# A list scheduler's table of durations and hops, replaced in a fused attention, expert and feed-forward kernel

## The chip, the cores and the metric

One core of one Trainium2 chip runs the whole kernel. The metric is the device time in microseconds (us). The time before is 1770.32 us, the median of three runs (1769.96 to 1772.51). The profile comes from one execution, with five engines: TensorE (PE) multiplies matrices, VectorE (DVE) and ScalarE (ACT) do element work, GpSimd (POOL) helps them, SyncE (SP) starts the transfers.

## The reference

Three stages follow each other, in float32, for 4 batches of 576 rows, 8 heads of 64:

```python
# attention without a seq x seq matrix; each half has its own softmax
q_s = exp(q - max(q, -1));  q_s /= sum(q_s, -1) + 1e-9        # over a row's 64 values
k_s = exp(k - max(k, seq)); k_s /= sum(k_s, seq) + 1e-9       # over the 576 rows
x   = einsum('bhsd,bhde->bhse', q_s, einsum('bhsd,bhse->bhde', k_s, v))   # -> 2304 x 512
# 8 experts, all of them for all rows; the gate is balanced 8 times
P = exp(x @ w_gate - max)
for _ in range(8):
    P /= P.sum(1, keepdims=True) + 1e-9;  P /= P.sum(0, keepdims=True) + 1e-9;  P *= 2304 / 8
y = sum(P[:, e:e+1] * (relu(x @ w1[e]) @ w2[e]) for e in range(8))        # 512 -> 1024 -> 512
# feed-forward with a hard swish
h = y @ w_in;  out = (h * clip(h + 3, 0, 6) / 6) @ w_out                  # 512 -> 2048 -> 512
```

## The kernel before, in words

The arithmetic is float32 made of float16 pieces: an operand is scaled by a power of two and split into a high and a low float16 part, and a product is three float16 products. The large products are done by blocks with seven block products in place of eight, so there are many sums and differences of blocks to form ahead of PE and behind it. Weights come to `raw`, are split by ACT (the high part) and DVE (the low part, a `scalar_tensor_tensor`, STT below) into `w1buf_79`/`w1buf_80` and `w2buf_81`/`w2buf_82`, and are ready one slice ahead of their use. Tokens come in strips of 384: a product `b<-xbuf,w1buf` is six matmuls of 128x384 into one of eight PSUM banks (`b_61` to `b_68`); ACT and DVE gather the banks into `ring_r`, split `ring_r` into `ring_h`, and the second products read `ring_h` and go to `acc`. Attention is done in two pairs of batches. The second pair's preparation lies beside the first expert work: the maximum of k over the sequence is a chain of four `tensor_max` on DVE (2048, 1024, 512 and 512 wide, out in `scr`; marked `1kmax`), four PE transposes of `scr` (`1ktr`), a reduction to `ring_c_109`, eight PE products with `units` that spread the result over the rows (`1kback`), two wide subtractions on DVE (`xbuf<-xbuf,b`, 2304 wide; `1ksub`), exponentials on ACT (`1kexp`) and a burst of 64x64 products on PE. The scale of a weight slice needs a sum of squares (ACT), a product with `identb` on PE that brings the partitions' values together (`b<-identb,ring_c`), and small DVE operations into `ring_ws`.

No engine reorders at run time: each executes its instructions in the order of the program. That order is worked out by the class `Planner`, in which every operation is first recorded, with what it reads and writes. `cost` (L177) gives an operation a duration from its shape; `hop` (L286) the time between the end of one operation and the start of a dependent one on another engine; `order` (L295) walks backwards to a due time for each operation, shifted for some by the tables EARLIER and LATER, and calls `lay` (L317) twice. `lay` is a list scheduler: it keeps the time at which each engine is free, takes the engine whose best ready operation can start first, and of operations that can start within 30 ns of each other the one due first. Its first pass lays what is not marked as fill; the second lays everything, and a fill operation (weight preparation, conversion of w_in and w_out) goes in where `following` finds that it delays nothing due. DVE and POOL operations that share a port carry a lock, and in the plan they exclude each other. `issue` (L444) then emits all in the planned order, and, in the plan's first 130 us, puts small filler matmuls (`b<-units,plus`, L2385) where the plan sees PE pause for over 400 ns, called warm in the code; they have no result. So the planned times decide nothing but the order and the fillers' number. What waits for what on the chip is set by semaphores.

Of the kernel before, what the change touches and what calls it, by code (L numbers as in the profile page):

```python
# [73 lines left out]
class Planner:  # L74
# [7 lines left out]
    HOP = 120.0  # L82
    MARGIN = 300.0
    NEAR = 4000.0
# [92 lines left out]
    def cost(self, eng, name, out, ins):  # L177
# [4 lines left out]
        if eng == "tensor":  # L182
            passes = 1.0
            if out.dtype == F32 and ins[0].dtype == F32:
                passes = 2.0 if name == "transpose" else 4.0 if ins[0].shape[0] > 64 else 1.5
            return 2.0 + n * 0.4167 * passes
        if eng == "scalar":
            return 170 + 0.8 * n if psum else (720 if n == 512 else 180 + 0.9 * n)
# [7 lines left out]
        if eng == "gpsimd":  # L196
            if big == 512 and len(out.shape) > 2:
                return 1610
            return 70 + (2.25 if len(ins) > 1 else 1.2) * big
# [86 lines left out]
    def hop(self, a, b):  # L286
        if a["eng"] == b["eng"] and a["eng"] != "sync":
            return 0.0
        if a["eng"] == "tensor":
            return 170.0 + self.HOP  # L290
        if a["eng"] == "sync":
            return a.get("land", 2500.0 + a["dma"] / 150.0)
        return self.HOP + (self.MARGIN if b["eng"] == "tensor" else 0.0)

# [22 lines left out]
    def lay(self, ops, first):  # L317
# [8 lines left out]
        lag = shift = pipe = 0.0  # L326
        gone = set()
# [14 lines left out]
        def following(q, t, d):  # L342
# [5 lines left out]
            for o in reversed(q[-24:]):  # L348
# [10 lines left out]
                u += o["dur"]  # L359
                v += o["dur"]  # L360
# [5 lines left out]
        def pick(e):  # L366
            f = free[e]
            c = []
            for o in waits[e]:
# [3 lines left out]
                if first and o["fill"] and e != "sync" and o["late"] + lag > s + self.NEAR:  # L373
                    room, fits = following(e, s, o["dur"])
                    if not fits:
                        s = max(s + 50.0, room + 1.0)
                    elif o["lock"]:
                        room, fits = following(other[e] + " lock", s, o["dur"])
                        if not fits:
                            s = max(s + 50.0, room + 1.0)  # L380
# [5 lines left out]
            if e not in ("tensor", "sync"):  # L386
                end = s + o["dur"]
# [5 lines left out]
        while len(result) < len(ops):  # L393
# [19 lines left out]
            end = s + o["dur"] * (1.0 if e == "tensor" else 1.05)  # L413
            if e == "sync":
                free[e] = s + 500.0
                pipe = max(pipe, s + 2000.0) + o["dma"] / 370.0
                o["land"] = pipe + 1500.0 - s
                end = s
            else:
                free[e] = end  # L420
            if o["lock"]:
                lock[e] = end
# [1996 lines left out]
```

## Time and profile before

| | |
|---|---|
| Runs (median, lowest, highest) | 1770.32, 1769.96, 1772.51 us |
| Span of the profiled execution, first to last instruction | 1768.3 us |
| PE busy | 1750.0 us (99%) |
| DVE busy | 1411.4 us (80%) |
| ACT busy | 1251.0 us (71%) |
| POOL busy | 588.0 us (33%) |
| Mean granted PE clock | 0.999 |

The page gives the profiled execution by its span; the median of the runs is 2.0 us above that, which is the start and the end around the instructions. A row of a timeline gives the start, the length and the number of instructions of a group; the length reaches to the modelled end of the last one. Since matmuls are pipelined, the start of the next row is often a better mark than the end of the last: six matmuls of 128x384 have a length of 1.14 us, and six more start 0.98 us behind them. An idle time stands in brackets behind a row, with what ended it. Filler matmuls count as busy in all views, so a stretch in which PE waits can read as 100% busy; they are told apart by their line, L2385.

### The profile page before, as it was taken

Reading aid. Unit: us, or ns where it says so; the run is one execution under the profiler, and the core shown is the slowest. Engines: PE = TensorE matmul, PEld = TensorE weight load, DVE = VectorE, ACT = ScalarE, POOL = GpSimd, SP = SyncE. Lnnn points to the kernel's source line nnn. Section 1 sums busy time; section 2 is a strip of 40 time slices with the busy share of each in tenths; the row PEclk is TensorE's granted clock in tenths of the full one; section 3 lists DMA queues with packets and bytes.
Section 4 is the critical chain, followed back from the end, with each engine's and each line's share of the span. In section 5 each row is a group of like instructions: output and inputs, shape, how many; then the busy total and the mean of one; then the engine's idle time right before and its main releaser. Section 6 shows DMA issues by size and latency. Waiting matters only on the chain.

```text
span 1768.3 us, 33908 instructions
## 1 busy us (share of the span) xinstructions
PE 1750.0 (99%) x13199; PEld 1218.1 (69%) x13199; DVE 1411.4 (80%) x2629; ACT 1251.0 (71%) x2807; POOL 588.0 (33%) x651
## 2 busy tenths in 40 slices
PE   7999999999999999999999999999999999999999
PEld 5555556777777777777777777777777555777776
DVE  7874877787888888888888888888888788777884
ACT  5856575667667686777778687768777677767673
POOL 3423343434444423232333322333323223223311
PEclk9999999999999999999999999999999999999999
DMA  9410322324242313020303122130312454402022
GB/s 293 121 69 1 117 84 74 99 98 154 98 161 96 111 37 105 25 87 25 119 21 119 37 93 63 49 105 25 105 49 93 87 100 136 150 25 87 1 87 84
DMA packets 103330, 154.25 MB, mean 87 GB/s; under 512 B 47744, under 2 KB 51840, under 8 KB 102912
## 3 DMA queue, kind: packets, MB, share of 16 engines
q1 hardware_dynamic: 103168, 152.08, 27.8%
q8 instruction: 103, 1.69, 0.4%
q14 instruction: 59, 0.48, 0.1%
HBM read 119.69 MB, written 24.12 MB: 81 GB/s over the span
## 4 chain that ended last, share of the span: by engine, by line
PE 96%; DVE 2%; issue 1%; DMA 1%; ACT 0%; POOL 0%; SPq 0%; DVEq 0%; POOLq 0%; ACTq 0%
PE b L472 95%; PE b L2385 1%; DMA xbuf<-in_k_dram 0%; DVE prob L472 0%; DVE acc L472 0%; DVE ring_r L472 0%; DVE xbuf L472 0%; DMA acc<-in_q_dram 0%; DVE ring_rs L472 0%; SPq L472 0%; ACT w2buf L472 0%; DVE scr L472 0%; DVE ring_cs L472 0%; POOL wtmp L472 0%; DVE ring_c L472 0%
## 5 line engine op out<-in xcount | busy, mean ns | idle before, releaser
L472 PE MATMUL b<-xbuf,w1buf 128*128 128x384 f16 x5040 | 910.6, 326 | 0.4 <-DVE ring_r L472 0.2
L472 PEld LDWEIGHTS <-w1buf 128*128 128x128 f16 x5040 | 491.5, 98 | 278.2 <-issue 1.8
L472 PE MATMUL b<-w2buf,ring_h 128*128 128x256 f16 (+2 forms) x3048 | 523.5, 308 | 0.0
L472 POOL TENSOR_TENSOR ring_h<-ring_r,ring_h 128x384 f16<-128x384 f32 x262 | 259.8, 993 | 693.4 <-ACT ring_h L472 632.7
L472 PEld LDWEIGHTS <-ring_h 128*128 128x128 f16 x3810 | 371.4, 98 | 155.9 <-issue 1.8
L472 ACT COPY b<-b 128x256 f32<-128x256 f32 (+1 forms) x686 | 253.8, 376 | 191.5 <-PE b L472 114.6
L472 DVE SCALAR_TENSOR_TENSOR acc<-b,ring_cf,acc 128x512 f32<-128x512 f32 x372 | 270.9, 746 | 120.7 <-PE b L472 94.3
L472 PEld LDWEIGHTS <-xbuf 128*128 128x128 f16 x3228 | 303.2, 98 | 75.5 <-DVE xbuf L472 1.1
L472 ACT ACTIVATE ring_r<-b 128x384 f32<-128x384 f32 x319 | 155.2, 488 | 94.9 <-PE b L472 87.7
L472 DVE SCALAR_TENSOR_TENSOR ring_r<-b,ring_r 128x384 f32<-128x384 f32 x215 | 118.7, 553 | 65.3 <-PE b L472 37.6
L472 PE MATMUL b<-xbuf 128*128 128x256 f16 (+1 forms) x1338 | 118.8, 251 | 2.2 <-issue 1.6
L472 POOL TENSOR_TENSOR raw<-raw 128x256 f32<-128x256 f32 (+1 forms) x119 | 102.0, 874 | 52.7 <-DVE w2buf L472 18.9
L472 POOL TENSOR_TENSOR ring_h<-scr,ring_h 128x384 f16<-128x384 f32 x40 | 38.8, 970 | 225.2 <-ACT ring_h L472 216.6
L472 ACT ACTIVATE ring_h<-ring_r 128x384 f16<-128x384 f32 x210 | 108.2, 521 | 7.7 <-DVE ring_r L472 5.4
L472 PE MATMUL b<-scr,xbuf 128*128 128x256 f16 x762 | 107.2, 273 | 0.1
L472 PE MATMUL b<-w2buf,xbuf 128*128 128x256 f16 x762 | 107.2, 273 | 0.0
L472 PE MATMUL b<-kvs,xbuf 128*128 128x256 f16 x762 | 107.2, 273 | 0.0
L472 PE MATMUL b<-xbuf,ring_h 128*128 128x256 f16 x468 | 91.2, 273 | 0.0
L472 DVE SCALAR_TENSOR_TENSOR acc<-b,ring_co,acc 128x512 f32<-128x512 f32 (+1 forms) x82 | 60.3, 741 | 27.5 <-PE b L472 25.7
L472 DVE TENSOR_TENSOR xbuf<-scr,xbuf 128x384 f16<-128x384 f32 x126 | 76.9, 635 | 6.5 <-ACT xbuf L472 6.3
L472 DVE SCALAR_TENSOR_TENSOR w1buf<-raw,ring_ws,w1buf 128x512 f16<-128x512 f32 x100 | 79.2, 825 | 3.1 <-ACT w1buf L472 2.7
L472 ACT ACTIVATE scr<-b 128x384 f32<-128x384 f32 x113 | 54.8, 488 | 37.2 <-PE b L472 36.6
(197 smaller groups left out, 2128.2 us busy)
## 6 DMA issues: line engine op xcount, KB each, us to landing
xbuf<-xkeep SPq DMA_DIRECT2D x119, 384.0 KB, 3.5
raw<-in_moe_w_dram SPq DMA_DIRECT2D x31, 1024.0 KB, 5.5
scr<-in_moe_w_in_dram SPq DMA_DIRECT2D x13, 512.0 KB, 3.7
scr<-in_moe_w_out_dram SPq DMA_DIRECT2D x12, 512.0 KB, 3.4
xkeep<-xbuf SPq DMA_DIRECT2D x2, 2688.0 KB, 9.0
xkeep<-xbuf SPq DMA_DIRECT2D x14, 384.0 KB, 8.4
out_dram<-acc SPq DMA_DIRECT2D x18, 256.0 KB, 2.0
raw<-win SPq DMA_DIRECT2D x4, 1024.0 KB, 5.4
```

The costliest lines, as they stand in the source:

```text
L472: f(*a, **k)
L2385: real.tensor.matmul(banks[t][:, : 2 * P], plus, some, start=True, stop=True, skip_group_check=True)
```

## The change

The table of durations and hops gets other numbers, and the scheduler tells two times apart. (1) The hop from DVE or ACT to another engine goes from 120 to 45 ns, from POOL to 95; a result for PE still adds MARGIN, 300 ns. From PE to another engine it is 165 ns and the hop of the receiver (45, or 95 for POOL), in place of 290. (2) `held`, which is new, is the time for which an operation keeps its engine (and the lock): its duration less 80 ns on DVE and ACT or 40 ns on POOL, times 1.01. Its result is there after the whole duration. Before, both were the duration times 1.05. (3) Durations: ACT's formula loses its special case at 512 and adds 90 ns for each further input; POOL's is 320+1.6n with two inputs and 220+0.88n with one, where it was 70+2.25n and 70+1.2n; PE's products on 64 rows get shorter. DVE's formula stays. (4) Transfers: at most eight are under way in the plan, with another rate and another latency. The operations are the same, 9017 in both; EARLIER and LATER stay, and the fillers go from 131 to 132.

```diff
@@ -79,8 +79,11 @@
...
     SLACK = 60000.0
-    HOP = 120.0
+    HOP = {"vector": 45.0, "scalar": 45.0, "gpsimd": 95.0, "tensor": 65.0, "sync": 120.0}
+    OVERLAP = {"vector": 80.0, "scalar": 80.0, "gpsimd": 40.0}
+    IN_FLIGHT = 8
     MARGIN = 300.0
+    SLOW = 1.01
@@ -182,10 +185,12 @@
...
             if out.dtype == F32 and ins[0].dtype == F32:
-                passes = 2.0 if name == "transpose" else 4.0 if ins[0].shape[0] > 64 else 1.5
+                passes = 2.0 if name == "transpose" else 4.0 if ins[0].shape[0] > 64 else 0.78
+            elif ins[0].shape[0] <= 64:
+                passes = 0.3
...
         if eng == "scalar":
-            return 170 + 0.8 * n if psum else (720 if n == 512 else 180 + 0.9 * n)
+            return (170 + 0.8 * n if psum else 180 + 0.88 * n) + 90 * (len(ins) - 1)
@@ -194,9 +199,7 @@
...
         if eng == "gpsimd":
-            if big == 512 and len(out.shape) > 2:
-                return 1610
-            return 70 + (2.25 if len(ins) > 1 else 1.2) * big
+            return 320 + 1.6 * big if len(ins) > 1 else 220 + 0.88 * big
@@ -287,10 +290,13 @@
...
         if a["eng"] == "tensor":
-            return 170.0 + self.HOP
+            return 165.0 + self.HOP[b["eng"]]
...
             return a.get("land", 2500.0 + a["dma"] / 150.0)
-        return self.HOP + (self.MARGIN if b["eng"] == "tensor" else 0.0)
+        return self.HOP[b["eng"]] + (self.MARGIN if b["eng"] == "tensor" else 0.0)
+
+    def held(self, o):
+        return max(o["dur"] - self.OVERLAP.get(o["eng"], 0.0), 40.0) * (1.0 if o["eng"] == "tensor" else self.SLOW)
@@ -324,6 +330,7 @@
...
         lag = shift = pipe = 0.0
+        landed = []
@@ -356,8 +363,8 @@
...
                     break
-                u += o["dur"]
-                v += o["dur"]
+                u += self.held(o)
+                v += self.held(o)
@@ -371,11 +378,11 @@
...
                 if first and o["fill"] and e != "sync" and o["late"] + lag > s + self.NEAR:
-                    room, fits = following(e, s, o["dur"])
+                    room, fits = following(e, s, self.held(o))
...
                     elif o["lock"]:
-                        room, fits = following(other[e] + " lock", s, o["dur"])
+                        room, fits = following(other[e] + " lock", s, self.held(o))
@@ -384,7 +391,7 @@
...
             if e not in ("tensor", "sync"):
-                end = s + o["dur"]
+                end = s + self.held(o)
@@ -410,16 +417,19 @@
...
             o["start"] = s
-            end = s + o["dur"] * (1.0 if e == "tensor" else 1.05)
+            end = s + o["dur"]
             if e == "sync":
+                if len(landed) >= self.IN_FLIGHT:
+                    s = max(s, landed[-self.IN_FLIGHT])
                 free[e] = s + 500.0
-                pipe = max(pipe, s + 2000.0) + o["dma"] / 370.0
-                o["land"] = pipe + 1500.0 - s
+                pipe = max(pipe, s + 1900.0) + o["dma"] / (310.0 if s < 4500.0 else 385.0)
+                landed.append(pipe + 200.0)
+                o["land"] = landed[-1] - s
...
             else:
-                free[e] = end
+                free[e] = s + self.held(o)
             if o["lock"]:
-                lock[e] = end
+                lock[e] = free[e]
...
             if e == "tensor":
```

Since the plan's numbers changed, most rows of the program change places: 1278 of PE's 2776 operations, 2378 of DVE's 2629, 2239 of ACT's 2628, 483 of POOL's 645 and 170 of SP's 339. Three places follow. In these rows a name such as `b_62<-xbuf,w1buf_79` is the tile written and the tiles read, and a count at the end means equal rows in succession.

PE, four transposes of the second pair's k maximum (`b_67<-units,scr`). Before, they stand late in the first expert work, between products with `w1buf_80`:

```order
L472 LDWEIGHTS w1buf_80
L472 MATMUL b_61<-xbuf,w1buf_80 128x384
L472 MATMUL b_67<-units,scr 128x128 x4
L472 LDWEIGHTS w1buf_80
L472 MATMUL b_62<-xbuf,w1buf_80 128x384
```

Now they stand behind a product with `w1buf_79` and two fillers:

```order
L482 LDWEIGHTS w1buf_79
L482 MATMUL b_62<-xbuf,w1buf_79 128x384
L2395 LDWEIGHTS plus
L2395 MATMUL b_68<-units,plus 128x256
L2395 LDWEIGHTS plus
L2395 MATMUL b_68<-units,plus 128x256
L482 MATMUL b_67<-units,scr 128x128 x4
L482 LDWEIGHTS w1buf_79
L482 MATMUL b_62<-xbuf,w1buf_79 128x384
```

The four transposes moved ahead of some twenty product groups; they keep their place in front of the eight products that spread the maximum.

DVE, the maximum's last two steps and the splits of `w1buf_80`. Before:

```order
L472 TENSOR_TENSOR scr<-scr 128x8x64
L472 SCALAR_TENSOR_TENSOR w1buf_80<-wtmp,ring_ws,w1buf_80 128x512
L472 SCALAR_TENSOR_TENSOR w1buf_80<-raw,ring_ws,w1buf_80 128x512
L472 SCALAR_TENSOR_TENSOR w1buf_80<-wtmp,ring_ws,w1buf_80 128x512
L472 SCALAR_TENSOR_TENSOR ring_r<-b_62,ring_r 128x384
L472 TENSOR_SCALAR ring_ws<-ring_c1i 128x1
L472 SCALAR_TENSOR_TENSOR w2buf_81<-acc,ring_ws,w2buf_81 128x512 x2
L472 SCALAR_TENSOR_TENSOR ring_r<-b_63,ring_r 128x384
L472 SCALAR_TENSOR_TENSOR ring_r<-b_62,ring_r 128x384
L472 SCALAR_TENSOR_TENSOR w2buf_81<-acc,ring_ws,w2buf_81 128x512 x2
L472 SCALAR_TENSOR_TENSOR w1buf_80<-raw,ring_ws,w1buf_80 128x512 x2
L472 TENSOR_TENSOR scr<-scr,xbuf 128x512
```

Now the maximum's last three steps (`scr<-scr 128x8x128`, `scr<-scr 128x8x64`, `scr<-scr,xbuf 128x512`) stand here, ahead of the splits:

```order
L482 TENSOR_REDUCE ring_c_108<-b_67 128x1
L482 TENSOR_TENSOR scr<-scr 128x8x128
L482 SCALAR_TENSOR_TENSOR ring_r<-b_62,ring_r 128x384
L482 TENSOR_SCALAR ring_c_108<-ring_c_108 128x1
L482 TENSOR_TENSOR scr<-scr 128x8x64
L482 SCALAR_TENSOR_TENSOR ring_h<-ring_r,ring_h 128x384
L482 TENSOR_SCALAR ring_c1i<-ring_c_108 128x1
L482 TENSOR_TENSOR scr<-scr,xbuf 128x512
L482 TENSOR_SCALAR ring_ws<-ring_c1i 128x1 x2
L482 SCALAR_TENSOR_TENSOR ring_r<-b_62,ring_r 128x384
```

and the splits stand around the two wide subtractions (`xbuf<-xbuf,b_68 128x2304`):

```order
L482 SCALAR_TENSOR_TENSOR w1buf_80<-raw,ring_ws,w1buf_80 128x512
L482 SCALAR_TENSOR_TENSOR w2buf_81<-acc,ring_ws,w2buf_81 128x512
L482 SCALAR_TENSOR_TENSOR w1buf_80<-wtmp,ring_ws,w1buf_80 128x512
L482 SCALAR_TENSOR_TENSOR w1buf_80<-raw,ring_ws,w1buf_80 128x512
L482 SCALAR_TENSOR_TENSOR ring_r<-b_62,ring_r 128x384
L482 TENSOR_TENSOR xbuf<-xbuf,b_68 128x2304
L482 SCALAR_TENSOR_TENSOR ring_r<-b_62,ring_r 128x384
L482 SCALAR_TENSOR_TENSOR ring_r<-b_63,ring_r 128x384
L482 TENSOR_TENSOR xbuf<-xbuf,b_68 128x2304
L482 SCALAR_TENSOR_TENSOR w1buf_80<-wtmp,ring_ws,w1buf_80 128x512
```

The two subtractions stood behind the splits and now stand ahead of the fourth `w1buf_80` split of this slice.

DVE in the middle of the expert stage, from the splits of the next slice's weights (`w1buf_79<-raw`) to the gather of `b_62` into `scr`, which frees a bank for PE. Before:

```order
L472 SCALAR_TENSOR_TENSOR ring_r<-ring_r 128x384
L472 SCALAR_TENSOR_TENSOR w1buf_79<-raw,ring_ws,w1buf_79 128x512
L472 SCALAR_TENSOR_TENSOR ring_r<-ring_r 128x384
L472 TENSOR_SCALAR ring_ws<-ring_c1i 128x1
L472 SCALAR_TENSOR_TENSOR w1buf_79<-raw,ring_ws,w1buf_79 128x512 x2
L472 SCALAR_TENSOR_TENSOR acc<-b_67,ring_cf,acc 128x512
L472 SCALAR_TENSOR_TENSOR acc<-b_66,ring_cf,acc 128x512
L472 SCALAR_TENSOR_TENSOR scr<-b_62,scr 128x384
L472 SCALAR_TENSOR_TENSOR w1buf_79<-raw,ring_ws,w1buf_79 128x512 x2
L472 TENSOR_TENSOR ring_r<-scr,ring_r 128x384
```

and now:

```order
L482 TENSOR_TENSOR xbuf<-ring_r,xbuf 128x384
L482 TENSOR_SCALAR ring_c1i<-ring_c_108 128x1
L482 TENSOR_TENSOR xbuf<-ring_r,xbuf 128x384
L482 TENSOR_SCALAR ring_ws<-ring_c1i 128x1
L482 TENSOR_TENSOR xbuf<-ring_r,xbuf 128x384
L482 TENSOR_TENSOR ring_r<-ring_r 128x384
L482 TENSOR_SCALAR ring_ws<-ring_c1i 128x1
L482 SCALAR_TENSOR_TENSOR w1buf_79<-raw,ring_ws,w1buf_79 128x512
L482 SCALAR_TENSOR_TENSOR acc<-b_67,ring_cf,acc 128x512
L482 SCALAR_TENSOR_TENSOR acc<-b_66,ring_cf,acc 128x512
L482 SCALAR_TENSOR_TENSOR w1buf_79<-raw,ring_ws,w1buf_79 128x512 x4
L482 SCALAR_TENSOR_TENSOR scr<-b_62,scr 128x384
```

The gather stood behind three of these splits and two `acc` additions, and now stands behind five of them, three `xbuf` subtractions and a sum as well.

## Rows read from the trace of the kernel before

**Rows 1.** The page: PE's busy time, and the chain that ended last.

```profile
PE 1750.0 (99%) x13199; PEld 1218.1 (69%) x13199; DVE 1411.4 (80%) x2629; ACT 1251.0 (71%) x2807; POOL 588.0 (33%) x651
...
PE 96%; DVE 2%; issue 1%; DMA 1%; ACT 0%; POOL 0%; SPq 0%; DVEq 0%; POOLq 0%; ACTq 0%
```

**Rows 2.** By stretch: start:end, length, each engine's busy us (instructions), clock, DMA.

```profile
0.00:20.00 20.00, 9.21 (x57) 6.15 (x58) 12.54 (x24) 5.77 (x12) 4.27 (x9) 0.96 0.93 331
...
20.00:40.00 20.00, 19.57 (x425) 15.26 (x422) 14.79 (x36) 15.98 (x25) 12.96 (x11) 0.95 0.92 240
...
40.00:60.00 20.00, 20.00 (x141) 12.83 (x140) 18.82 (x40) 17.97 (x44) 6.01 (x7) 1.00 0.82 231
...
800.00:1000.00 200.00, 199.99 (x1536) 149.82 (x1535) 168.23 (x305) 150.74 (x357) 62.96 (x70) 1.00 0.20 61
```

**Rows 3.** Timeline of PE, 49-72 us: start, length, line, operation, count.

```profile
51.91 0.60 PE L2385 MATMUL b<-units,plus 128*128 128x256 f16 x4
...
56.30 0.38 PE L2385 MATMUL b<-units,plus 128*128 128x256 f16 x2
...
58.52 0.71 PE L2385 MATMUL b<-units,plus 128*128 128x256 f16 x5
...
61.02 0.60 PE L2385 MATMUL b<-units,plus 128*128 128x256 f16 x4
...
67.31 4.05 PE L472 MATMUL b<-w2buf,ring_h 128*128 128x512 f16 x18
```

**Rows 4.** Timeline of DVE, 52 to 88 us.

```profile
52.42 1.37 DVE L472 TENSOR_TENSOR scr<-scr 128x1024 f32<-128x1024 f32 x1
...
58.67 0.75 DVE L472 SCALAR_TENSOR_TENSOR w1buf<-raw,ring_ws,w1buf 128x512 f16<-128x512 f32 x1
...
59.34 0.68 DVE L472 TENSOR_TENSOR scr<-scr 128x512 f32<-128x512 f32 x1
...
69.24 1.21 DVE L472 TENSOR_TENSOR scr<-scr,xbuf 128x512 f32<-128x512 f32 x1
...
82.67 5.02 DVE L472 TENSOR_TENSOR xbuf<-xbuf,b 128x2304 f32<-128x2304 f32 x2
```

**Rows 5.** Timeline of ACT, 52 to 57 us.

```profile
54.75 0.63 ACT L472 ACTIVATE w1buf<-raw 128x512 f16<-128x512 f32 x1
...
56.28 0.52 ACT L472 ACTIVATE ring_h<-ring_r 128x384 f16<-128x384 f32 x1
```

**Rows 6.** Timeline of POOL, 68 to 70 us.

```profile
68.73 1.17 POOL L472 TENSOR_TENSOR raw<-raw,wtmp 128x256 f32<-128x256 f32 x1
```

**Rows 7.** Timeline of PE, 78 to 95 us.

```profile
78.98 0.60 PE L472 MATMUL b<-units,scr 128*128 128x128 f32 x4
...
81.46 1.09 PE L472 MATMUL b<-units,ring_c 128*64 128x128 f32 x16
...
93.77 1.45 PE L472 MATMUL b<-xbuf 64*64 64x65 f32 x83 [1.55 <-issue]
```

**Rows 8.** Timeline of PE at the balancing of the gate.

```profile
205.99 0.39 PE L472 MATMUL b<-ring_cs,units 128*128 128x8 f32 x2 [0.28 <-DVE ring_cs L472]
...
210.15 0.39 PE L472 MATMUL b<-ring_cs,units 128*128 128x8 f32 x2 [0.51 <-DVE ring_cs L472]
```

**Rows 9.** Timeline of PE in the expert stage.

```profile
867.61 0.27 PE L472 MATMUL b<-lg,ring_h 128*128 128x256 f16 x1
...
879.74 1.14 PE L472 MATMUL b<-xbuf,w1buf 128*128 128x384 f16 x6
```

**Rows 10.** Timeline of DVE in the expert stage.

```profile
868.53 1.41 DVE L472 SCALAR_TENSOR_TENSOR acc<-b,ring_cf,acc 128x512 f32<-128x512 f32 x2 [1.14 <-ACT b L472]
...
877.00 1.41 DVE L472 SCALAR_TENSOR_TENSOR acc<-b,ring_cf,acc 128x512 f32<-128x512 f32 x2 [0.23 <-PE b L472]
...
878.33 0.55 DVE L472 SCALAR_TENSOR_TENSOR scr<-b,scr 128x384 f32<-128x384 f32 x1
```

**Rows 11.** The page's costliest groups: DVE's sums of 384.

```profile
L472 DVE SCALAR_TENSOR_TENSOR ring_r<-b,ring_r 128x384 f32<-128x384 f32 x215 | 118.7, 553 | 65.3 <-PE b L472 37.6
```

## The prediction, made before the changed kernel ran

> **What bounds the kernel now.** I read the page's busy times and chain first, then the busy time by stretch, then the timelines of PE, DVE and ACT in the stretches where PE does not run through. PE is busy for 1750.0 of 1768.3 us and holds 96% of the chain that ended last [rows 1]: whatever the new order does counts only if it takes a wait of PE away or makes one. The stretches say where waits can go. In the first 20 us PE is busy for 9.21 us and in the next 20 for 19.57, at granted clocks of 0.96 and 0.95; from 40 us it reads full at 1.00 [rows 2]. But DVE and ACT are nearly full there too, 18.82 and 17.97 of 20 us, and the 15 fillers that PE executes between 51.9 and 61.5 us (4, 2, 5 and 4) are waits in disguise: PE's real work could not start in these slots [rows 3]. In the expert stage DVE is busy for 168.23 of 200 us and PE for 199.99 [rows 2]: there is some slack on DVE, but an order that pushes other work ahead of a result that PE needs can use it up in one place. So PE bounds, and DVE's and ACT's order decides what little PE waits.
>
> **What the new numbers do to the plan.** A DVE operation of 512 columns with a PSUM or two SBUF inputs costs 743 ns by the unchanged formula; the plan kept DVE for 743 x 1.05 = 780 ns, and now keeps it for (743 - 80) x 1.01 = 670. The rows bear the new value out: two such operations from 868.53 are over after 1.41 us, so the second starts 0.66 behind the first if it lasts 0.75 [rows 10]. The plan also believes that a result of DVE or ACT reaches PE 75 ns sooner, and MARGIN stays. So it sees more room on DVE and ACT, fills it with fill work and work of later due times, and puts PE's consumers closer behind. That is nearer to the trace in the mean, and leaves less reserve where a single operation takes longer than its formula.
>
> **The sum, place by place.** The sum is made against the profiled span of 1768.3 us; the median of the runs is 2.0 us above it, and I add the sum to the median, 1770.32.
>
> *The head, 0 to 45 us: 0, from -2 to +1.5.* The reductions of the second k maximum move ahead of two q maxima, an exponential moves back, one weight split and three small operations go in front of the scaling that PE's first forming products wait for (about 1 us later on DVE). PE has 11.2 us of not busy in 40 [rows 2], so there is something to win, but by 45 us PE stands behind the same splits and forming operations on DVE and ACT, whose number is unchanged and which fill DVE for 18.82 of 20 us. I take nothing.
>
> *45 to 56 us: -0.15.* The first scale product comes ahead of one product group, and the four fillers at 51.91 [rows 3] shrink, of which a third of their 0.44 us (4 at the 109 ns that the planner counts) is taken; the work on DVE and ACT ahead of it is the same.
>
> *56 to 72 us: +2.4, from 1.5 to 3.7.* This is the place that decides. Before, PE executes the four transposes of the k maximum at 78.98, with the maximum done at 69.24 + 1.21: over 8 us of reserve [rows 4, 7]. Now they stand right behind a product that ends at about 56.3 (as the one ahead of the two fillers there did [rows 3]), and the maximum's last three steps are drawn together on DVE. Worked from the rows of before: the second step starts at 52.42, now some 0.3 later for a reduction put ahead of it, and holds DVE for 1.30, to 54.05; a 384-wide sum at 0.47 from start to start (553 ns lasting [rows 11]) and a small operation follow; the third step, 0.68 lasting [rows 4], goes to about 55.4; a low part of `ring_h`, which needs its high part from ACT, to 55.8; a small one; the fourth from 56.0 to 56.6 if it costs what the third does, or 57.2 at the 1.21 of its own row. PE waits for 0.4 (1.0) in front of the transposes. Next, ACT's four squares for the second scale have moved behind the `ring_h` activation that ran at 56.28; the last of them ran at 54.75 [rows 5], ends now at about 58.95, and the scale product cannot start before 59.2. The plan has four fillers there. Then come the eight spreading products (1.02 us, 81.46 to 82.48 [rows 7]), one block product on either side.
>
> The third wait is the longest. The fourth split of `w1buf_80` now stands behind both wide subtractions. DVE's work from the scale product to its end: a reduction and four small operations (0.8), four splits (0.67 from start to start with 0.75 lasting, one longer: 2.8), three 384-wide sums (1.4), two subtractions (5.02 [rows 4]) and the split itself (0.7): 10.7 us from 59.45, so 70.2 without a wait; the sums wait for PE's products in between, I take 0.9 for that, and PE ends the block product that needs the split at 72.1. The plan has put 11 fillers (1.2 us) in front of it. Before, the same product gave way to the next group at 67.31 [rows 3], and 1.45 us for transposes and spreading and 0.98 for a block product are now done ahead of it, which makes 69.74 for equal work: +2.4. The lower end has no wait of the sums (+1.5), the upper one the fourth step and the splits at contended durations, as in the row at 69.24 (+3.7). Nothing gives it back: the burst that follows is not waited for by anything but its own start, and the 1.55 us "issue" in it at 93.77 [rows 7] has no operation behind it that moves.
>
> The row at 69.24 is 0.53 us longer than the same form at 59.34, and POOL ran a sum of two SBUF tiles from 68.73 to 69.90 beside it [rows 4, 6]. The Trainium skill (SBUF — State Buffer, "Who interferes with whom") says that a DVE instruction with two SBUF inputs contends with a GpSimd instruction that reads SBUF, and that the one that comes second is blocked altogether. By that rule the price of the fourth step depends on what POOL does at 56 us: 0.6 in place of 0 comes on top of the 2.4, and the result would be 1774.4; the trace agrees in this one pair of rows.
>
> *72 to 200 us: 0, up to +1.3.* The k exponentials and the subtractions are now done some 15 us before the burst that needs them, which it did not wait for before either.
>
> *The gate's balancing, 200 to 240 us: 0, within 0.5.* Eight sums on PE wait for DVE's column sums; two of the waits show, 0.28 and 0.51 us [rows 8]. The new order puts more of PE's products between them and more conversion work on DVE as well; counted by rows' durations, both grow alike.
>
> *560 to 1550 us: +1.3, from 0 to 3.4.* The order on DVE now takes some results behind more work than PE has in between. The clearest place: before, DVE goes from the `acc` additions at 868.53 to the gather at 878.33, which ends at 878.88, with 1.0 us of waits [rows 10], the last 0.23, so 9.3 us of work, and PE's products from 867.61 to 879.74 lie beside it [rows 9], 12.1 us. Now DVE has two more splits (0.75 to 1.2 each), four 384-wide operations (0.47 each), a low part (0.9), a 512-wide conversion (1.1) and one more 384-wide sum in this loop, about 6 us more, 15.3 in all; PE has two block products of 0.98 and two of 0.66 more, 15.4 in all. With the 0.92 from PE's product to DVE's start and some 0.2 for the release, DVE is late by about 0.9 us. Ten more places of this kind come out at 0.05 to 0.6 us by the same count, together 3.4; on the other side some 1.2 us of such excess in the old order near 1332 and 1357 goes. Fill work may run beside a wait at several of them, so I take a good half of the net.
>
> Sum: 0 - 0.15 + 2.4 + 0 + 0 + 1.3 = 3.5 us; 1770.3 + 3.5 = **1773.8 us**. With the terms at their ends together, -0.15 + 1.5 + 0 - 0.5 - 2 = -1.2 and -0.15 + 3.7 + 1.3 + 0.5 + 3.4 + 1.5 = +10.3.
>
> **Rivals.** (a) *No net change.* For it: PE is full almost everywhere, each new wait is below 1 us, and the old order had waits of its own that vanish. Against it: the transposes' reserve falls from 8 us to nothing, by the order alone. Worked out: 1.5 at 56 to 72, nothing in the expert stage, -0.8 for the two waits at the gate: +0.6, 1770.9.
>
> (b) *Faster: PE's old waits go.* The durations are nearer to the trace, so the order loses waits that the plan did not see: 2 to 3 us of the 11.2 in the head, the 0.8 at the gate, 1.2 near 1357, and half of the 1.6 us of fillers at 51.9 to 61.5 (15 at 109 ns) [rows 2, 3, 8]. Against it: DVE and ACT are the cause in the head, and they are full. Worked out: -2.5 - 0.8 - 1.2 - 0.8 = -5.3, about 1765.
>
> (c) *Clearly slower: contention in the tight order.* The plan takes 80 ns off each DVE operation and gives no reserve for a blocked one; where POOL works beside it, a DVE operation took 1.21 for 0.68 [rows 4]. If each of the eleven places of the expert stage meets one such, that is 11 x 0.53 = 5.8 on top of 3.4, and with 3.7 at 56 to 72 it makes +13; half of it, +7, gives 1777 and is where I would look first. It decides from the point at which one DVE operation in each loop is blocked.
>
> That the change does not do what it says is out: the order differs on all five engines.
>
> **How the numbers follow.** Less than 0.2%, 3.5 us, cannot be told from no change here: the bounds are 1766.8 and 1773.9. Chances: the forecast 0.42 (its own range 1772 to 1776, so half of it counts as same), (a) 0.27, (b) 0.17, (c) 0.14. That makes faster 0.16 from (b), same 0.21 + 0.26 from the forecast and (a), slower 0.21 + 0.14 and a little of the rest: 0.16, 0.46, 0.38. The range for 8 in 10 is 1767 to 1779; it leaves out the far halves of (b) and (c).
>
> **What would show it.** The forecast is right if PE's row of the four transposes stands near 57 us with 0.3 to 1.0 idle, due to DVE `scr`, if the 11 fillers near 70 us stand in front of a wait for `w1buf`, and if short idles due to DVE `scr`, `xbuf` or `acc` add up to 1 to 3 us between 560 and 1550. It is wrong if PE's real work by 75 us is not behind the old trace (then the chain on DVE was shorter than I made it), or if the head alone gains or loses over 2 us.

## The result, and the profile after

The changed kernel takes 1793.58 us (median; 1793.15 to 1794.29) against 1770.14 us for the kernel before, a ratio of 1.0132 with a 95% interval of 1.0118 to 1.0146: 23.4 us slower, where 3.5 us were forecast. The span grew from 1768.3 to 1792.5 us.

The page's lines that answer to [rows 1] (busy time; shares of the chain that ended last by engine, and by line):

```profile
PE 1756.1 (98%) x13200; PEld 1219.3 (68%) x13200; DVE 1392.6 (78%) x2629; ACT 1245.1 (69%) x2807; POOL 580.5 (32%) x651
...
PE 82%; DMA 7%; DVE 6%; ACT 4%; issue 1%; POOL 0%; SPq 0%; DVEq 0%; ACTq 0%
PE b L482 82%; DMA raw<-in_moe_w_dram 3%; DVE w1buf L482 1%; DMA raw<-wout 1%; ACT w1buf L482 1%; DVE scr L482 1%; ACT w2buf L482 1%; DVE acc L482 1%; DVE ring_r L482 1%; DMA xbuf<-scr 1%; ACT scr L482 1%; ACT ring_h L482 1%; ACT ring_r L482 1%; DVE xbuf L482 1%; DMA acc<-in_q_dram 0%
```

PE's share of the chain fell from 96% to 82%, and a new name stands second: 7% are DMA, with the loads of the expert weights into `raw` first among them. The 7% are not what was lost, since the chain counts a load from its issue on. The stretches that answer to [rows 2], and one behind them (columns as there):

```profile
0.00:20.00 20.00, 10.26 (x61) 6.64 (x61) 13.74 (x25) 5.86 (x12) 4.39 (x9) 1.00 0.94 329
20.00:40.00 20.00, 17.50 (x372) 13.93 (x372) 16.57 (x33) 15.09 (x23) 13.20 (x11) 0.91 0.75 192
40.00:60.00 20.00, 18.71 (x163) 11.89 (x164) 18.87 (x34) 15.33 (x38) 6.36 (x6) 1.00 0.94 280
...
600.00:800.00 200.00, 196.43 (x1497) 146.09 (x1495) 156.02 (x289) 144.26 (x342) 57.00 (x67) 1.00 0.25 79
800.00:1000.00 200.00, 200.00 (x1538) 150.06 (x1536) 166.25 (x314) 152.23 (x363) 64.03 (x74) 1.00 0.20 67
```

In the first 60 us PE is busy for 46.47 us, against 48.78 before. The stretch of 600 to 800 us has PE at 196.43 of 200, where the kernel before had 200.00; the one of 800 to 1000 us, which I had read for the expert stage, is still full. A single stretch is no sample of a stage.

To place the loss I compared, in both traces, the times at which PE had done the same amount of real work (its matmuls without fillers). Behind the old trace by: 2.3 us at 45 us of the old trace, 1.8 at 56, about 5 at 72 (4.5 to 5.1, as the work is weighed, since the mix of products differs there), 6.8 at 95, 7.6 at 135, 8.8 at 300, 13.3 at 465, 18.0 at 800, 19.9 at 1300 and 24.2 at the end. So 8.8 us are lost ahead of 300 us, and 15.4 us behind. What PE waited for behind 300 us (engine, what it waited for, us in all, times, longest):

```profile
PE b L482 <- ACT b L482: 6.5, 6, 1.7
PE b L482 <- ACT ring_r L482: 6.1, 5, 1.6
PE b L482 <- DVE ring_r L482: 1.4, 3, 0.8
PE b L482 <- ACT scr L482: 0.6, 1, 0.6
PE b L482 <- DVE acc L482: 0.4, 1, 0.4
```

and before:

```profile
PE b L472 <- DVE xbuf L472: 0.5, 1, 0.5
PE b L472 <- DVE ring_r L472: 0.2, 1, 0.2
```

15.0 us against 0.7, and most of it (13.2) on ACT. The longest are 1.6 and 1.7 us. One of 1.14 us, with the chain ahead of it (start, us, what):

```profile
459.29 0.60 PE L482 MATMUL b<-scr,xbuf 128*128 128x256 f16 x4 [1.14 <-ACT b L482]
```

```profile
449.64 8.21 DMA raw<-in_moe_w_dram
...
457.87 0.72 ACT w2buf L482 x2
458.59 0.38 ACT ring_r L482
458.97 0.27 ACT b L482
```

and ACT's timeline there:

```profile
457.87 0.63 ACT L482 ACTIVATE w2buf<-raw 128x512 f16<-128x512 f32 x1 [2.88 <-DMA raw<-in_moe_w_dram]
...
458.50 0.47 ACT L482 ACTIVATE ring_r<-b 128x384 f32<-128x384 f32 x1
458.87 0.37 ACT L482 COPY b<-b 128x256 f32<-128x256 f32 x1
```

A load of 1 MB is issued at 449.64 and is there at 457.85. ACT stands idle for 2.88 us in front of the first square of these weights, and behind this square, in ACT's fixed order, stand the gather into `ring_r` and the copy of a bank that PE waits for. Of the load's 8.21 us in the chain, PE lost 1.14 here. So a wait of ACT, which is busy for 69% of the span, became a wait of PE.

### The profile page after: what moved, and what is told of

Its sections match the earlier page's. It is cut to its first block, busy times and chain, and to the rows that moved or that the text cites. A ratio compares the mean times of both kernels' runs of the same rounds, so it can differ in the third digit from the quotient of the medians.

```text
span 1792.5 us, 33906 instructions
## 1 busy us (share of the span) xinstructions
PE 1756.1 (98%) x13200; PEld 1219.3 (68%) x13200; DVE 1392.6 (78%) x2629; ACT 1245.1 (69%) x2807; POOL 580.5 (32%) x651
## 4 chain that ended last, share of the span: by engine, by line
PE 82%; DMA 7%; DVE 6%; ACT 4%; issue 1%; POOL 0%; SPq 0%; DVEq 0%; ACTq 0%
PE b L482 82%; DMA raw<-in_moe_w_dram 3%; DVE w1buf L482 1%; DMA raw<-wout 1%; ACT w1buf L482 1%; DVE scr L482 1%; ACT w2buf L482 1%; DVE acc L482 1%; DVE ring_r L482 1%; DMA xbuf<-scr 1%; ACT scr L482 1%; ACT ring_h L482 1%; ACT ring_r L482 1%; DVE xbuf L482 1%; DMA acc<-in_q_dram 0%
## 5 line engine op out<-in xcount | busy, mean ns | idle before, releaser
L482 PE MATMUL b<-xbuf,w1buf 128*128 128x384 f16 x5040 | 905.1, 326 | 13.3 <-ACT ring_r L482 6.3
L482 POOL TENSOR_TENSOR ring_h<-ring_r,ring_h 128x384 f16<-128x384 f32 x262 | 255.9, 978 | 740.0 <-ACT ring_h L482 674.0
L482 ACT ACTIVATE ring_h<-ring_r 128x384 f16<-128x384 f32 x210 | 109.4, 521 | 17.8 <-DVE ring_r L482 14.9
L482 POOL TENSOR_TENSOR raw<-raw 128x256 f32<-128x256 f32 (+1 forms) x119 | 94.4, 817 | 21.3 <-issue 13.4
L482 ACT CAST ring_h<-ring_r 128x384 f16<-128x384 f32 x133 | 67.2, 508 | 20.7 <-DVE ring_r L482 19.5
L482 DVE SCALAR_TENSOR_TENSOR w1buf<-raw,ring_ws,w1buf 128x512 f16<-128x512 f32 x100 | 75.2, 786 | 3.8 <-ACT w1buf L482 3.3
L482 ACT CAST xbuf<-scr 128x384 f16<-128x384 f32 x132 | 65.8, 506 | 16.9 <-DVE scr L482 16.3
```

Source lines behind the costliest of these rows:

```text
L482: f(*a, **k)
```

## The experiments

The theory after the first look (T): the transfer part of the change makes the loss. By the old plan a 1 MB load is there 2.0 + 2.83 + 1.5 = 6.3 us after its issue, by the new one 1.9 + 2.72 + 0.2 = 4.8. On the chip the 39 loads into `raw` took from 4.86 to 12.6 us, with 5.6 us for the median of the 31 from the expert weights. The plan put ACT's squares where it thought the data there. The rival (R): hops and holding, packed without reserve, as my prediction had it. All times below are medians; the ratio is to runs of the kernel before on the same chip. Losses by stretch are read from one profile for each kernel; that of e1 comes from its fastest run, 2.9 us below its median, and that of e5 from its slowest, 2.6 above.

| Run | us | ratio, 95% interval |
|---|---|---|
| e1: changed, transfers as before | 1778.33 | 1.0041, 1.0026 to 1.0056 |
| e2: before, transfers new | 1779.71 | 1.0051, 1.0036 to 1.0066 |
| e3: changed, landing 1.3 us later | 1778.96 | 1.0047, 1.0032 to 1.0062 |
| e4: changed, hops and holding as before | 1783.90 | 1.0075, 1.0058 to 1.0092 |
| e5: before, hops and holding new | 1782.41 | 1.0066, 1.0050 to 1.0082 |
| e6: before, durations new | 1788.27 | 1.0097, 1.0082 to 1.0112 |
| e7: before, landing 1.5 us later | 1772.94 | 1.0010, 1.0000 to 1.0019 |
| e8: changed, two POOL sums moved | 1793.68 | 1.0132, 1.0117 to 1.0148 |
| e9: before, HOP 125 | 1772.37 | 1.0007, 0.9998 to 1.0016 |
| e10: before, landing 1.5 us later from 100 us on | 1767.83 | 0.9984, 0.9975 to 0.9993 |
| e11: e1, old numbers for the first 700 operations | 1772.34 | 1.0011, 1.0002 to 1.0020 |
| e12: changed, a split moved behind the scaling | 1794.15 | 1.0129, 1.0115 to 1.0143 |

**e1, the changed kernel with the old transfers.**

```diff
-                if len(landed) >= self.IN_FLIGHT:
-                    s = max(s, landed[-self.IN_FLIGHT])
                 free[e] = s + 500.0
-                pipe = max(pipe, s + 1900.0) + o["dma"] / (310.0 if s < 4500.0 else 385.0)
-                landed.append(pipe + 200.0)
-                o["land"] = landed[-1] - s
+                pipe = max(pipe, s + 2000.0) + o["dma"] / 370.0
+                o["land"] = pipe + 1500.0 - s
```

> The changed kernel with the transfer model of the kernel before (no limit of eight, 2.0 us + bytes/370 + 1.5 us to the landing); hops, holding and durations stay new. Theory T (the plan lets a 1 MB weight load land 4.8 us after its issue, it takes 4.9 to 8.2, and ACT's squares then stand in front of gathers that PE needs): the waits of PE behind late loads after 300 us, about 14.8 us in all, go; 1779 us, from 1776 to 1782. Rival R (the tight order on DVE and ACT, by 80 ns less holding and 75 ns less hop, makes the waits): 1790 or more.

It came out at 1778.33 us: 15.3 of the 23.4 us are gone, as T had it, and R falls as the main cause. ACT's waits on loads of weights (the same columns as above), before:

```profile
ACT w1buf L472 <- DMA raw<-in_moe_w_dram: 7.3, 4, 5.5
...
ACT w2buf L472 <- DMA raw<-wout: 2.4, 1, 2.4
ACT w2buf L472 <- DMA raw<-in_moe_w_dram: 2.1, 2, 1.4
```

in the changed kernel:

```profile
ACT w1buf L482 <- DMA raw<-in_moe_w_dram: 14.1, 7, 5.5
...
ACT w2buf L482 <- DMA raw<-in_moe_w_dram: 11.2, 7, 3.0
...
ACT w2buf L482 <- DMA raw<-wout: 6.9, 4, 2.4
...
ACT w1buf L482 <- DMA raw<-win: 1.2, 1, 1.2
```

and in e1:

```profile
ACT w1buf L479 <- DMA raw<-in_moe_w_dram: 6.7, 2, 6.3
...
ACT w2buf L479 <- DMA raw<-wout: 2.0, 2, 1.5
...
ACT w1buf L479 <- DMA raw<-win: 0.2, 1, 0.2
```

11.8 us in 7 waits, 33.4 in 19, 8.9 in 5. By the amount of work done, e1 loses 1.2 us behind 300 us, the changed kernel 15.4.

**e2, the kernel before with the new transfers alone**, the converse:

> The kernel before with nothing but the new transfer model. T: 12 to 15 us slower than before, about 1783 us, with 20 or more of the 39 loads of raw whose first square starts within 0.1 us of the landing (8 in the kernel before, 23 in the changed one). R: within 3 us of before, 1773 or less.

```diff
...
+                if len(landed) >= self.IN_FLIGHT:
+                    s = max(s, landed[-self.IN_FLIGHT])
                 free[e] = s + 500.0
-                pipe = max(pipe, s + 2000.0) + o["dma"] / 370.0
-                o["land"] = pipe + 1500.0 - s
+                pipe = max(pipe, s + 1900.0) + o["dma"] / (310.0 if s < 4500.0 else 385.0)
+                landed.append(pipe + 200.0)
+                o["land"] = landed[-1] - s
```

9.8 us slower than the kernel before, outside what either theory had, but on T's side. ACT's waits on weights, in e2:

```profile
ACT w1buf L477 <- DMA raw<-in_moe_w_dram: 19.7, 9, 5.7
...
ACT w2buf L477 <- DMA raw<-wout: 4.4, 2, 2.2
ACT w2buf L477 <- DMA raw<-in_moe_w_dram: 4.4, 6, 1.6
```

28.5 us in 17 waits, and 18 of the 39 loads (T: 20 or more) have their first square within 0.1 us of the landing (8 in the kernel before, 24 in the changed one, 6 in e1). That is about as many waits as in the changed kernel, but PE took less of it: the new transfers cost 9.8 us alone and 15.3 with the new hops, holding and durations. The two parts do not add up; that they make each other dearer, as more of PE's inputs stand close behind a square, is argued from this and was not tried by itself.

**e3, one constant of it.**

```diff
-                landed.append(pipe + 200.0)
+                landed.append(pipe + 1500.0)
```

> The changed kernel with one number more: a transfer lands 1.5 us behind the pipe in place of 0.2, as in the kernel before; the limit of eight and the new rates stay. T: it is the landing alone, so nearly all of e1's gain comes back: 1779 to 1782 us. If the limit of eight or the rates carry it: 1788 or more. R: 1790 or more.

1778.96 us, as e1: 14.6 of the 23.4 us are gone. So it is the 1.3 us of the landing, neither the limit of eight nor the rates. All that PE waits for behind 300 us in e3:

```profile
PE b L482 <- ACT b L482: 2.2, 2, 1.5
```

Behind 300 us e3 loses 0.8 us. Ahead of it, it loses 8.5, about as much as the changed kernel (8.8): what the landing brings lies in the later part.

**e4, hops and holding as before.**

```diff
-    HOP = {"vector": 45.0, "scalar": 45.0, "gpsimd": 95.0, "tensor": 65.0, "sync": 120.0}
-    OVERLAP = {"vector": 80.0, "scalar": 80.0, "gpsimd": 40.0}
+    HOP = {"vector": 120.0, "scalar": 120.0, "gpsimd": 120.0, "tensor": 120.0, "sync": 120.0}
+    OVERLAP = {}
...
-    SLOW = 1.01
+    SLOW = 1.05
...
-            return 165.0 + self.HOP[b["eng"]]
+            return 170.0 + self.HOP[b["eng"]]
...
-            end = s + o["dur"]
+            end = s + o["dur"] * (1.0 if e == "tensor" else self.SLOW)
```

> The changed kernel with the hops of the kernel before (120 ns, 170 behind PE) and with engines held for the duration times 1.05, results at that time too; durations and transfers stay new. T: little changes, 1786 to 1794 us. R: 1772 to 1776.

1783.90 us, 9.7 us of the 23.4 gone: more than T allowed, less than R needs. **e5 and e6** try these parts alone.

> The kernel before with the new hops and the new holding alone; durations and transfers as before. Theory T now (transfers carry some 15 of the 23 us, the hops and the holding make them dearer, since the work that waits behind a late load is packed closer): with loads that are not believed early, 1771 to 1776 us, the loss ahead of 60 us. Rival (the hops and the holding are the second cause by themselves): 1778 or more.

> The kernel before with the new durations of ACT, POOL and PE alone. T: within 3 us of before, 1768 to 1773. Rival (the durations make the 4 us by which durations and transfers together, 1783.9, are slower than transfers alone, 1779.7): 1773 to 1775.

e5 has the edit of e4 the other way round in the kernel before; e6 has the new lines of `cost` there:

```diff
...
-            return 170 + 0.8 * n if psum else (720 if n == 512 else 180 + 0.9 * n)
+            return (170 + 0.8 * n if psum else 180 + 0.88 * n) + 90 * (len(ins) - 1)
...
-            return 70 + (2.25 if len(ins) > 1 else 1.2) * big
+            return 320 + 1.6 * big if len(ins) > 1 else 220 + 0.88 * big
```

T missed both, and not by little: 1782.41 us, which is in e5's rival's range, and 1788.27, which is above e6's rival's too, while e1, which has both pieces, takes 1778.33. Each new piece alone costs 10 to 18 us, and two together cost less. In its profile e5 loses 14.9 us, most of it ahead of 110 us (10.4; 2.5 behind 300). e6 loses 9.2 by 135 us and 8.6 behind 300, with ACT's waits on `raw` at 11.6 us, no more than the 11.8 of the kernel before; PE's largest waits behind 300 us in e6:

```profile
PE b L472 <- DVE xbuf L472: 2.0, 3, 1.4
PE b L472 <- ACT ring_r L472: 1.9, 3, 1.2
PE b L472 <- ACT b L472: 1.7, 6, 0.4
```

So there is a loss behind 300 us that longer waits for these loads do not explain, and DVE's differences into `xbuf` and ACT's results share in it. Which duration brings it was not taken apart, and stays open.

**e9, a control.** With every single piece slower, the order before might only be a lucky one, which any new number spoils.

```diff
-    HOP = 120.0
+    HOP = 125.0
```

> A control: the kernel before with one hop number 5 ns larger (120 to 125), which says nothing new of the chip but changes the list schedule's choices. Theory S (the order before sits in a good spot, and any other plan loses several us in the first 60 us, where DVE and ACT bound): 1773 to 1780 us, with the loss ahead of 60 us. Rival (only numbers that are wrong for the chip cost time): 1769 to 1771.5.

1772.37 us, between the two ranges, and the interval takes in no change, though the order differs on all engines: theory S falls in its strong form. This plan, which is different but believes nothing new of the chip, costs 0 to 3 us; the pieces of the change cost 10 to 18. One control does not show how much another order could lose by chance, so that e5 and e6 lose because their numbers are wrong for the chip is argued.

**e7 and e10, landings later still.**

```diff
-                o["land"] = pipe + 1500.0 - s
+                o["land"] = pipe + 3000.0 - s          # e7
+                o["land"] = pipe + (3000.0 if s > 100000.0 else 1500.0) - s      # e10
```

> The kernel before with landings 1.5 us later still (1 MB: 7.8 us after its issue, about the longest that the traces show). T: the waits of ACT on loads that are left in the kernel before go, and with them the 1.2 us at 1356: 1768 to 1770 us. Rival (a later landing pushes weight work against its due time): 1772 or more.

> The kernel before with landings 1.5 us later for transfers that the plan issues behind 100 us; the start is planned as before. If the late-load waits are what is left there: the 2.5 us that the kernel with later landings everywhere gains behind 135 us come without its loss in the head: 1767.5 to 1769 us, faster than both kernels. If that gain came from the head's shift: 1770 to 1772.

e7 came out 0.1% slower, in the rival's range and above T's. Its profile is 5.4 us behind at 110 us, in the head, and gains 1.7 from there to the end; that weight work was pushed against its due time, the rival's reason, is not shown. e10 keeps the old plan for the start and is faster than both kernels: 1767.83 us, a ratio of 0.9984 (0.9975 to 0.9993). PE's waits behind 300 us in e10:

```profile
PE b L472 <- ACT b L472: 0.3, 1, 0.3
PE b L472 <- DVE xbuf L472: 0.2, 1, 0.2
```

ACT waits once for a load into `raw`, for the first weights (6.0 us), and for no other. At the start it is level with the kernel before (0.2 us at 135 us). It gains 1.5 us at 200 to 220, where PE waited for the gate's sums [rows 8], loses 1.0 between 465 and 800, and gains 1.3 at 1355 to 1380, where four squares of w_out stood in succession on ACT ahead of a copy that PE needed. Neither gain is a wait for a load, and e1, e7 and e11 gain 1.0 to 1.4 at each of the two places as well: they are weak spots of the old order that several other plans avoid. That e10 is faster is measured; that the later landing makes it so is not shown.

**e11, the new numbers behind the start only.** e1, with `cost`, `hop` and holding as before for operations recorded as the first 700 (attention and the first expert work):

```diff
...
+            return 290.0 if a["n"] < 700 else 165.0 + self.HOP[b["eng"]]
...
+        return (120.0 if a["n"] < 700 else self.HOP[b["eng"]]) + (self.MARGIN if b["eng"] == "tensor" else 0.0)
...
+            end = s + o["dur"] * (1.05 if o["n"] < 700 and e != "tensor" else 1.0)
...
```

> The changed kernel with the old transfers, and with the old hops, holding and durations for the first 700 recorded operations (attention and the first expert work); the new numbers rule the rest. If the new numbers cost time only in the head (there 4.2 us by 135 us with the old transfers): 1770 to 1772.5 us. If they cost it in the expert stage as well: 1774 or more.

1772.34 us, as expected for a cost in the head alone: 6.0 us less than e1, and level with the kernel before at 135 us (0.7 ahead). With transfers as before, what the new hops, holding and durations cost is lost at the start. Behind it they bring nothing either: e11 loses 2.2 us from 135 us to its end. Taken off one after the other, then, the 23.4 us are 15.3 for the transfers (e1), 6.0 for the other new numbers at the start (e11), and 2.1 that are left, which is within the 0 to 3 of e9. In another order the parts would weigh differently, as e2, e5 and e6 show.

**e8 and e12, contention with POOL.** In the changed kernel the fourth step of the k maximum stands beside two sums on POOL. e8 moves these two (by their numbers) behind the next POOL operation:

```diff
+        late = [o for o in ops if o["n"] in (445, 446)]
+        ops = [o for o in ops if o["n"] not in (445, 446)]
+        k = next(i for i, o in enumerate(ops) if o["n"] == 467) + 1
+        ops[k:k] = late
```

> The changed kernel with one move by hand: the two sums of weights on POOL that run beside the third and fourth step of the k maximum (56.99 us, two in succession) go behind the ring_h subtraction that follows them (59.12); all other engines keep their order. If contention with POOL makes the step at 58.56 last 1.15 us and the ring_h operation ahead of it 1.08, both fall to 0.6 to 0.75, PE's four transposes start at 58.7 to 59.0 in place of 59.76, and PE's real work is 0.7 to 1.1 us earlier until 72 us; 1792 to 1793.5 us in all, as later waits take some of it. If not, the two stay above 1.0.

It failed: the step got longer. DVE and POOL in e8:

```profile
58.53 1.36 DVE L486 TENSOR_TENSOR scr<-scr,xbuf 128x512 f32<-128x512 f32 x1
```

```profile
58.43 0.92 POOL L486 TENSOR_TENSOR ring_h<-ring_r,ring_h 128x384 f16<-128x384 f32 x1 [0.30 <-ACT ring_h L486]
```

The POOL operation that was behind the two sums moved up beside the step in their place. The other kernels settle what it costs: with POOL idle the step lasts 0.68 to 0.69 us (e1, e2, e6, e9), beside POOL 1.15 to 1.40 in eight kernels and 0.67 and 0.68 in two (e3, e4). In e3, where it lasts 0.67, PE's work is about as far behind at 72 us as in the changed kernel, so this contention does not decide the loss there. **e12** does the same for one split on DVE (343) and the POOL subtraction that waits for it (356), behind the scaling (299):

> The changed kernel with one move by hand: the weight split on DVE at 37.59 and the POOL subtraction at 38.48 that waits for it go behind the scaling at 38.63; other engines keep their order. If the split, and contention with POOL (the scaling lasts 1.27 for 0.35 before), delay PE's forming products, they start near 38.0 in place of 39.95. Then either the gain is gone by 46 us, as the prediction had it (the splits bound DVE anyway), or PE's work at 56 us is 1 to 2 us earlier. In all 1790.5 to 1793.5.

Changed kernel, DVE's scaling and POOL's subtraction:

```profile
38.63 1.27 DVE L482 TENSOR_SCALAR xbuf<-xbuf,sx 128x256 f32<-128x256 f32 x1
```

```profile
38.48 1.27 POOL L482 TENSOR_TENSOR raw<-raw,wtmp 128x512 f32<-128x512 f32 x1 [6.42 <-DVE mx L482]
```

and in e12, the scaling with the five splits behind it, and POOL:

```profile
39.24 0.35 DVE L486 TENSOR_SCALAR xbuf<-xbuf,sx 128x256 f32<-128x256 f32 x1
39.51 4.42 DVE L486 SCALAR_TENSOR_TENSOR w1buf<-raw,ring_ws,w1buf 128x512 f16<-128x512 f32 x5
```

```profile
40.40 1.65 POOL L486 TENSOR_TENSOR raw<-raw,wtmp 128x512 f32<-128x512 f32 x1 [7.30 <-DVE w1buf L486]
```

With POOL idle the scaling takes 0.35 us, beside the subtraction 1.27. The other traces agree: 0.35 with POOL idle in nine of the 14 kernels, 1.27 beside that subtraction in the other five. And now the splits take 4.42 us for five, where they took 0.75 and 2.73. So the contention was shown, and it moved on. This profile was already 1.6 us later when DVE began its stretch of work (35.90 against 34.31); PE's products behind the scaling start at 39.70, which is near the 38.0 that was expected when the 1.6 are taken off. From the start of the stretch to PE's first `w1buf` products it took 11.85 us against 12.95. The gain of 1.1 us did not fade by 56 us; at 60 us, behind the transposes' wait, the two profiles are level, and at the end nothing is left of it: 1794.15 us, above the range.

The Trainium skill (SBUF — State Buffer, "Who interferes with whom") has it that a DVE instruction with two SBUF inputs contends with a GpSimd instruction that reads SBUF, and that `tensor_scalar` can contend too; the traces agree, with 1.27 against 0.35 us for a `tensor_scalar`, and 1.15 and 1.36 us for the fourth step of the k maximum against the 0.68 of the third, the same form, in [rows 4].

## Why the prediction was wrong

*The transfers, which it did not price.* The step that failed is the sum's silence on part (4) of the change. Of transfers it says nothing; its place "560 to 1550 us" has +1.3 from packed DVE work, and 240 to 560 us has no term. Measured are 15.4 us from 300 us on. The old transfers take 15.3 us away (e1), and 1.3 us on the landing alone 14.6 (e3). The row was there to be read, on the page of the kernel before (KB each, median us from issue to landing):

```profile
raw<-in_moe_w_dram SPq DMA_DIRECT2D x31, 1024.0 KB, 5.5
```

That is above the 4.8 of the new plan, and ACT waited for such loads in 7 places already. Its row on PE in the expert stage, 199.99 of 200, was right and said nothing of that.

*The mechanism of that stage.* Its worked example, DVE's loop from 868.53 to 878.88 [rows 9, 10], gave 0.9 us; between 800 and 1000 us PE waited for nothing. PE's waits on DVE from 300 us on are 1.8 us in all, on `ring_r` and `acc`, against 0.7 before. That looks near the +1.3, but e3, which has the new hops, holding and durations with the later landing, has no wait of PE on DVE there, and between 560 and 1550 us neither e1 nor e3 loses anything (0.1 and 0.7 us gained). So the +1.3 did not show by itself, and the likeness is luck.

*56 to 72 us, +2.4.* PE lost about 3 us there (from 1.8 to between 4.5 and 5.1). PE's timeline in the changed kernel (the two fillers, the transposes, the 11 fillers, and a wait further on), DVE's and POOL's:

```profile
58.09 0.38 PE L2395 MATMUL b<-units,plus 128*128 128x256 f16 x2
59.76 0.66 PE L482 MATMUL b<-units,scr 128*128 128x128 f32 x4 [1.29 <-DVE scr L482]
...
72.47 1.36 PE L2395 MATMUL b<-units,plus 128*128 128x256 f16 x11
...
83.61 1.14 PE L482 MATMUL b<-xbuf,w1buf 128*128 128x384 f16 x6 [1.55 <-DVE ring_r L482]
```

```profile
56.89 0.68 DVE L482 TENSOR_TENSOR scr<-scr 128x512 f32<-128x512 f32 x1
57.50 1.08 DVE L482 SCALAR_TENSOR_TENSOR ring_h<-ring_r,ring_h 128x384 f16<-128x384 f32 x1
...
58.56 1.15 DVE L482 TENSOR_TENSOR scr<-scr,xbuf 128x512 f32<-128x512 f32 x1
...
73.32 0.74 DVE L482 SCALAR_TENSOR_TENSOR w1buf<-wtmp,ring_ws,w1buf 128x512 f16<-128x512 f32 x1
...
81.34 1.75 DVE L482 TENSOR_REDUCE ring_qm<-acc 128x24 f32<-128x1536 f32 x1 [2.18 <-DMA acc<-in_q_dram]
```

```profile
56.99 2.17 POOL L482 TENSOR_TENSOR wtmp<-wtmp,raw 128x256 f32<-128x256 f32 x2
```

The transposes waited for the last step in `scr` and the 11 fillers stand in front of the product that needs the split behind both subtractions, as written. The first wait was 1.29 us, above the 0.4 to 1.0: the fourth step lasted 1.15 (forecast: 0.68, or 1.21 at the upper end) and the `ring_h` operation ahead of it 1.08, where the same form took 0.55 at 78.62, with POOL idle. The 1.15 and the 1.08 were beside POOL. The split behind both subtractions ended at 74.06, where the forecast had the product that needs it done at 72.1.

*72 to 200 us, 0.* It was 3.0 to 3.6, to 8.1 in all. At 83.61 PE waits 1.55 us: DVE's q maximum stood idle for 2.18 us for a load of q that landed at 81.12, 3.36 us after its issue, and PE's input stood behind it. That has the same form, a transfer and what is queued behind its reader. But with the landing alone put back (e3) the loss ahead of 300 us stays at 8.5 us, so that the new landing time makes this wait is not shown.

*The head, 0.* It was 2.3 us at 45 us, one profile against one, outside the -2 to +1.5 and past the prediction's own sign of 2 us, and 1.8 by 56. "By 45 us PE stands behind the same splits" was the wrong argument: where DVE is full, a delay ahead of it stays, as e12's profile has it (11.85 against 12.95, kept until 56). And the scaling itself took 0.9 us longer, beside POOL. With transfers as before, old numbers for the first 700 operations, attention and the first expert work, take 6.0 us away (e11), where the sum had 2.3 for all places ahead of 200 us.

*The rivals.* (c), the worst case, named contention at 13 us; what happened is worse, and e3 takes most of it away without touching DVE's or POOL's numbers. No rival held transfers.

## What to carry to other kernels

Where in-order engines follow a plan, ask of each number whether it errs early or late: a landing that is believed early puts the reader in front of other work on its engine, and all of it waits. The two landings of this case err by about as much on either side of the measured median of 5.6 us (4.8 and 6.3), and 1.3 us of the difference cost 14.6 us (e3). One that is believed later still, 7.8 us, cost 0.1% where the start was planned with it (e7) and came with a gain of 0.16% where it was not (e10). Price every edit of a change from a row, also the one on an engine that is far from bounding. The median is not the number to aim at where the prices of the two errors differ.

## What the runs showed of the hardware

A 1 MB load into `raw` took 4.86 to 8.21 us from issue to landing in the changed kernel's expert stage, beside other transfers. POOL's elementwise operations lengthen a DVE operation beside them by up to 0.9 us (0.35 to 1.27), and in both tries here moving one of the two moved the collision. Not every DVE operation beside POOL is lengthened: the third step in the changed kernel took 0.68 us beside POOL's sums (the lines at 56.89 and 56.99 above), as in the kernel before with POOL idle [rows 4]. The times vary: e7's ten runs spread over 5.1 us in all (1769.86 to 1774.99), and e12's profile entered the same stretch of DVE work 1.6 us later than the changed kernel's, behind the same instructions in the same order, so differences of a microsecond or two ahead of 60 us, read from single profiles, are not certain.
